# A gated-attention and feed-forward kernel on one core: gate sums worked out once and repeated over partitions by DMA, and attention on TensorE in one run per half block

## The chip, the cores and the metric

One core of a Trainium2 chip. The core has TensorE (matmul; PE in the profile, its weight loads PEld), VectorE (DVE), ScalarE (ACT), GpSimd (POOL) and SyncE (SP), which here only issues DMAs. The metric is device microseconds of one execution. Three runs of the kernel before gave 494.70, 497.48 and 496.63 us, a median of 496.63.

## The reference

A recurrent attention over 4 batches, 8 heads, 768 tokens and a head size of 40, then a feed-forward layer over the 4 x 768 tokens of 320 features, through 2048 hidden units:

```python
for t in range(S):
    m_new = np.maximum(f_gate[:, :, t] + m, i_gate[:, :, t])
    f_stab = np.exp(f_gate[:, :, t] + m - m_new)
    i_stab = np.exp(i_gate[:, :, t] - m_new)
    m = m_new
    C = f_stab * C + i_stab * np.einsum('bhd,bhe->bhde', vt, kt)
    n = f_stab * n + i_stab * kt
    h_tilde = np.einsum('bhde,bhe->bhd', C, qt)
    nq = np.einsum('bhd,bhd->bh', n, qt)[:, :, None]
    y[:, :, t] = sigmoid(o_gate) * h_tilde / np.maximum(np.abs(nq), 1.0)
...
h = x @ w_in
sp = np.maximum(h, 0.0) + np.log1p(np.exp(-np.abs(h)))
return (h * erf(sp)) @ w_out
```

The two weight matrices are double precision; everything else is float32.

## The kernel before

**Attention** works in chunks of L = 128 tokens. There are 6 chunks (c) of 4 batches (b), so 24 steps s = 4c + b. Inside a chunk the recurrence becomes a product of matrices: for tokens t and u with u <= t, the weight of u in t is exp(cum[t] + a[u]) times q[t]k[u], where cum is the running sum of the log of f_stab from the chunk's start and a the rest of the gates' terms. Whatever came before the chunk is in `state`, and enters with the factor exp(cum[t]). The gates of a chunk are worked out by `gate_chunk`: a scan for m (L314), differences on GpSimd (L322, L323), a scan for cum (L329), the rest (L334, L335), an exp (L341), and a split of the results into three bf16 parts (L351 to L353), of which `rhs` lays some on other partitions with twelve small DMAs (L363).

A step's operations, under the names that the code gives them, are: loads of q and k (`load`, L387) and of k, v and the output gate (`loadv`, L393, L394); `rows` (GpSimd, L403) and `pe` (TensorE, L413; L415 too for c = 0), which build cum[t] + a[u] in PSUM out of the bf16 parts; `ex` (ScalarE, L422), two exps of 128x512; `sel` (GpSimd, L427), which clears u > t; `S` (TensorE), which for c > 0 first multiplies `selP` (L443; the prediction calls this part pq) to repeat exp(cum) over partitions, and then forms k q (L449); `vg` (v times the last column of weights); `w` (VectorE, L464); `qa` (VectorE, L473: q times exp(cum)); `ph` (TensorE, L482 to L493: state times q, plus w times v, and, but for the last chunk, the new part of the state); `sa` and `sk` (the state's update); `yg` (VectorE, L524 to L528), `y` and `yy` (GpSimd, L532, L538), which divide and gate; `tr` (TensorE, L544: three transposes); and `xh`, `xl` (L557, L561), which split the transposed result into two parts that TensorE multiplies separately.

**The feed-forward layer** works on blocks of two steps (256 tokens), each in two half blocks; there are 24 such phases f. A phase has four ups (`up`, L675: 16 matmuls of 256 columns) and four downs (`dn`, L737 to L740: 12 of 320), and between them `hb` (copy out of PSUM), `sp` and `er` (softplus and erf on ScalarE), `mu` (VectorE), `gh` and `gl` (a split into two parts). Phases 0 to 3 are blocks 0 and 1, so phase 4 is the first that needs the attention of chunk 1. The weights come as 22 tiles of doubles (`win`, `tail`, `wout`) and are decoded into two float32 parts by `val` (ScalarE), `dec` (VectorE, L580, L581), `hi` (ScalarE, L586) and `lo` (L592, on GpSimd or, where `LO_DVE` names it, on VectorE).

**The order** of all this is written by a planner in the kernel (`Plan`) when the program is built: each operation is given an engine, a cost, what it waits for, which buffers it holds and, for TensorE, a due time. `issue` simulates the engines with these costs and picks, whenever an engine is free, the operation with the least slack. `NUDGE` shifts the slack of single operations, `SLOTS` and `CAPS` count buffers, and `AHEAD` says behind which phase's exps a step's exps stand on ScalarE. The engines then work through their lists strictly in order, and all DMAs go through SyncE's queue in order.

## Time and profile before

| | |
|---|---|
| median of the three runs | 496.63 us |
| profiled execution | 496.05 us, its span 494.3 us |
| instructions | 14040 |
| GpSimd busy | 113.4 us, 23% of the span |
| moved by DMA | 39.40 MB, on average 80 GB/s |
| chain that ended last | TensorE 78%, VectorE 7%, DMA 6%, ScalarE 5% |

The profile is of one execution. A busy time is the sum of an engine's instructions; TensorE's matmuls overlap, so what one costs is read from the distance of starts. The slices cut the span into forty pieces of 12.4 us. The rows on which the prediction rests are shown there.

### The profile page before, as it was taken

The page shows a single profiled execution, that of the slowest core. Times are in us where ns is not written, and L with a number is a line of the kernel's source. Part 1 is how long each engine was busy: PE and PEld are TensorE (multiplying, and loading weights), DVE is VectorE, ACT ScalarE, POOL GpSimd, SP SyncE. Part 2 cuts the span into 40 slices and gives each one's busy share as a digit, 9 for nine tenths or more (in the row PEclk, how much of TensorE's full clock was granted, in tenths as well). Part 3 has the DMA queues.
Part 4 walks back from the last instruction along what each step waited for, and adds up shares of the span by engine and source line. Part 5 has one row for each costly group of instructions (what it writes and reads, how often), then busy time and mean ns, then how long its engine had stood idle before and what let it go on. Part 6 is the DMA issues. An engine that isn't in the chain of part 4 may idle for free.

```text
span 494.3 us, 14040 instructions
## 1 busy us (share of the span) xinstructions
PE 464.1 (94%) x6120; PEld 442.2 (89%) x6120; DVE 327.4 (66%) x562; ACT 333.6 (67%) x412; POOL 113.4 (23%) x187
## 2 busy tenths in 40 slices
PE   2787869799999999999999999999999999999997
PEld 1677769689999999999999999999999999999997
DVE  3787978587685666957675975765864754755541
ACT  4568898985494696567575666666656666667571
POOL 6684453242511011111011211001111001000000
PEclk9998989859999999999999999999999999999999
DMA  7999926123051203212203033203020000000000
GB/s 212 265 324 255 216 92 223 36 77 103 5 174 57 76 7 101 75 43 73 76 16 91 2 93 89 76 16 91 0 88 19 1 15 15 2 15 15 1 27 28
DMA packets 21221, 39.40 MB, mean 80 GB/s; under 512 B 3304, under 2 KB 12520, under 8 KB 21160
## 3 DMA queue, kind: packets, MB, share of 16 engines
q1 hardware_dynamic: 21160, 38.51, 27.2%
q8 instruction: 48, 0.79, 0.7%
q14 instruction: 13, 0.11, 0.1%
HBM read 34.45 MB, written 3.93 MB: 78 GB/s over the span
## 4 chain that ended last, share of the span: by engine, by line
PE 78%; DVE 7%; DMA 6%; ACT 5%; issue 2%; SPq 1%; POOL 0%; ACTq 0%; DVEq 0%
PE h L675 31%; PE po L737 12%; PE po L740 11%; PE po L738 11%; PE pa L449 4%; PE pa L482 3%; PE pa L486 2%; DMA raw<-in_w_out_dram 2%; DMA qk<-in_qk_dram 2%; DVE bits L580 2%; DVE bits L581 2%; PE pa L413 2%; PE pa L544 1%; DMA raw<-in_w_in_dram 1%; PE pa L493 1%
## 5 line engine op out<-in xcount | busy, mean ns | idle before, releaser
L675 PE MATMUL h<-xh,wh 128*128 128x256 f32 x576 | 164.2, 293 | 3.6 <-ACT wh L586 2.4
L675 PE MATMUL h<-xl,wh 128*128 128x256 f32 x576 | 159.7, 285 | 1.3 <-DVE xl L561 1.3
L737 PE MATMUL po<-woh,gh 128*128 128x320 f32 x384 | 119.7, 323 | 0.9 <-ACT woh L586 0.9
L675 PEld LDWEIGHTS h<-xh,wh 128*128 128x128 f32 x576 | 111.7, 194 | 6.7 <-ACT wh L586 2.6
L738 PE MATMUL po<-wol,gh 128*128 128x320 f32 x384 | 114.8, 311 | 1.2 <-POOL wol L592 1.2
L675 PEld LDWEIGHTS h<-xl,wh 128*128 128x128 f32 x576 | 111.8, 194 | 1.9 <-DVE xl L561 1.5
L675 PE MATMUL h<-xh,wl 128*128 128x256 f32 x384 | 109.8, 286 | 1.3 <-POOL wl L592 1.3
L686 DVE COPY hb<-h 128x512 f32<-128x512 f32 x72 | 49.6, 689 | 65.5 <-PE h L675 65.4
L694 ACT ACTIVATE e<-hb 128x1024 f32<-128x1024 f32 x48 | 50.0, 1056 | 63.3 <-DVE hb L686 45.8
L737 PEld LDWEIGHTS po<-woh,gh 128*128 128x128 f32 x384 | 72.8, 190 | 4.4 <-ACT woh L586 1.2
L675 PEld LDWEIGHTS h<-xh,wl 128*128 128x128 f32 x384 | 74.5, 194 | 1.6 <-POOL wl L592 1.6
L738 PEld LDWEIGHTS po<-wol,gh 128*128 128x128 f32 x384 | 72.9, 190 | 1.5 <-POOL wol L592 1.4
L740 PE MATMUL po<-woh,gl 128*128 128x320 f32 x384 | 72.4, 311 | 0.0
L702 DVE TENSOR_TENSOR hb<-e,hb 128x1024 f32<-128x1024 f32 x48 | 57.6, 1225 | 21.3 <-ACT e L698 20.7
L427 POOL TENSOR_SCALAR_AFFINE_SELECT dm<-dm 128x512 f32<-128x512 f32 x48 | 30.8, 663 | 139.3 <-ACT dm L422 139.1
L707 ACT ACTIVATE gh<-hb 128x1024 fp32r<-128x1024 f32 x48 | 50.6, 1058 | 16.3 <-DVE hb L702 15.8
L740 PEld LDWEIGHTS po<-woh,gl 128*128 128x128 f32 x384 | 60.8, 189 | 0.0
L712 DVE TENSOR_TENSOR gl<-hb,gh 128x1024 fp32r<-128x1024 f32 x48 | 59.2, 1236 | 1.5 <-ACT gh L707 1.4
L532 POOL TENSOR_TENSOR kvo<-kvo,den 128x320 f32<-128x320 f32 x24 | 21.7, 906 | 128.9 <-DVE kvo L528 128.8
L698 ACT ACTIVATE e<-e 128x1024 f32<-128x1024 f32 x48 | 48.7, 1052 | 0.3
L694 ACT ACT_TABLE_LOAD x25 | 32.1, 1283 | 4.1 <-DVE hb L686 3.7
L464 DVE TENSOR_TENSOR dm<-pa,dm 128x512 f32<-128x512 f32 x48 | 30.9, 683 | 5.1 <-PE pa L449 4.1
(78 smaller groups left out, 607.3 us busy)
## 6 DMA issues: line engine op xcount, KB each, us to landing
...
raw<-in_w_in_dram SPq DMA_DIRECT2D x8, 512.0 KB
...
```

Source lines behind the costliest of these rows:

```text
L427: nc.gpsimd.affine_select(out=v.w[j], in_=v.w[j], pattern=[[0, NPR], [1, L]], compare_op=ALU.is_ge, fill=0.0, base=0, channel_multiplier=-1)
L464: nc.vector.tensor_tensor(v.w[j], v.ps[j], v.w[j], op=ALU.mult)
L675: nc.tensor.matmul(V.h[i][:, n % 2 * T:(n % 2 + 1) * T], w, m, start=(q == 0), stop=(q == len(ops) - 1))
L686: nc.vector.tensor_copy(V.hb[:, i * 512:(i + 1) * 512], V.h[i])
L694: nc.scalar.activation(V.e, V.hb, AF.Softplus)
L698: nc.scalar.activation(V.e, V.e, AF.Erf)
L702: nc.vector.tensor_tensor(V.hb, V.e, V.hb, op=ALU.mult)
L707: nc.scalar.activation(V.gh, V.hb, AF.Copy)
L712: nc.vector.tensor_tensor(V.gl, V.hb, V.gh.bitcast(F32), op=ALU.subtract)
L737: nc.tensor.matmul(K.po[b], V.gh[:, ts], woh[:, w], start=start, stop=False)
L738: nc.tensor.matmul(K.po[b], V.gh[:, ts], wol[:, w], start=False, stop=False)
L740: nc.tensor.matmul(K.po[b], V.gl[:, ts], woh[:, w], start=False, stop=stop)
```

## The change

- The gates of chunks 1 to 5 are worked out once, on 32 partitions (one for a batch and head) and 768 columns: `lscan`, `lg`, `lsum`, `lrest`, `gexp`. cum and exp(cum) are written to DRAM (`cum_dr`, `dec_dr`). a is transposed by five matmuls (`at`) into `aT`, with tokens on partitions. Chunk 0 keeps its own gates and its `pe`; the clearing of u > t is added there as a matmul of a mask.
- For c > 0 `pe`, `rows`, `rhs`, and the product with `selP` are gone. `bq` reads 8 rows of cum into all 128 partitions (`dm`, 512 KB), and `dq` reads exp(cum) into 104 (`dq`, 208 KB). `add` on GpSimd adds a, then come one exp and one select over 1024 columns.
- `ph` puts its new state's part in the PSUM bank of its output.
- From step 8 on, `merge` makes one TensorE operation of tr of step s - 2, S of step s and ph of step s - 1, so S is one run ahead of its own ph.
- The planner's costs for TensorE's changes from one kind of work to another, its due times, the order of exps on ScalarE (`CHAIN` in place of `AHEAD` and `GATE`), the choice of engine for some operations (`HB_ACT`, `LO_DVE`, `VG_POOL`, `SK_ACT`, new `GL_POOL`), the buffers and `NUDGE` are changed.

```diff
-FIRST = 30.8
-PHASE = 18.0
-BEHIND = 1.3
+FIRST = 11.8
+PHASE = 17.5
+BEHIND = 1.32
...
-HB_ACT = {0, 1, 2, 3, 4, 6}
+HB_ACT = {0, 4, 6}
...
-LO_DVE = {'i01', 'i30', 'i31', 'o0', 'o2', 'o6'}
+LO_DVE = {'o1', 'o6', 't0'}
+CHAIN = [
+    ('ex', 0, 0), ('ex', 0, 1), ('ex', 1, 0), ('ex', 1, 1), ('ex', 2, 0), ('ex', 2, 1), ('ex', 3, 0), ('ex', 3, 1),
...
+GL_POOL = {2, 4}
+CLUSTER = 8
+PREFER = 16.6
...
+    @make('lscan', 'DVE', 3.2, after=[lload, p_small], new=[gmb], use=[gib, gfb])
+    def lscan():
+        late.m = row("late")
+        nc.vector.tensor_copy(late.m[:, 0:1], m0[0:R])
+        nc.vector.tensor_tensor_scan(out=late.m[:, 1:S + 1], data0=late.f[:, 0:S], data1=late.i[:, 0:S], initial=m0[0:R],
+                                     op0=ALU.add, op1=ALU.max)
...
+    @make('lsum', 'DVE', 3.2, after=[lg, p_lones], new=[gcb], use=[gfb, gyb])
...
+    @make('gexp', 'ACT', 0.85, after=[lsum], use=[gcb, gfb], table=('exp',))
+    def gexp():
+        nc.scalar.activation(late.f[:, 0:S], late.c[:, 0:S], AF.Exp)
+
+    def kept(name, t, src, after, buf):
+        @make(name, 'SP', 0.5, kb=100.0, after=after, use=[buf])
+        def put():
+            nc.sync.dma_start(t.rearrange("c b h l -> (b h) c l"), src()[:, 0:S].rearrange("p (c l) -> p c l", l=L))
+        return put
...
+    @make('at', 'PE', 0.5, after=[lrest, p_ident], new=[atb], use=[gib], mode=3)
+    def at_():
+        late.a = bank(NC - 1, R)
+        for c in range(1, NC):
+            nc.tensor.transpose(late.a[:, c - 1], late.i[:, c * L:(c + 1) * L], ident[0:R, 0:R])
...
+            @make(f'bq{s}', 'SP', 0.5, after=[p_cum], kb=512.0, new=[dmb])
+            def bq():
+                v.dm = new(sb, [128, H, L], F32, "dm")
+                v.w = ofj(v.dm)
+                nc.sync.dma_start(v.dm, cum_dr[c, b:b + 1].to_broadcast([128, H, L]))
+
+            @make(f'dq{s}', 'SP', 0.9, after=[p_dec], kb=208.0, new=[dqb])
+            def dqp():
+                v.dq = new(sb, [128, NPR, L], F32, "dq")
+                for j in range(2):
+                    n = 64 if j == 0 else D
+                    nc.sync.dma_start(v.dq[64 * j:64 * j + n],
+                                      dec_dr[c, b:b + 1].rearrange("o (p j) l -> o j p l", j=2)[:, j].to_broadcast([n, NPR, L]))
+
+            @make(f'add{s}', 'POOL', 2.7, after=[bq, p_at], use=[dmb])
+            def addp():
+                nc.gpsimd.tensor_tensor(v.dm, v.dm, aT[:, c - 1, 8 * b:8 * b + 8].unsqueeze(2).to_broadcast([128, H, L]), op=ALU.add)
...
+    for s in range(CLUSTER, B * NC + 1):
+        plan.merge(f'X{s}', [*([step[s - 2].tr] if s > CLUSTER else []), *([step[s].S] if s < B * NC else []), step[s - 1].ph_])
```

Three places show what moves. TensorE, at S of step 12, before (L443 is the product with selP, L449 is S, L737 and L738 begin a down):

```order
L443 LDWEIGHTS selP
L443 MATMUL pa<-splB_71,selP 128x128
L449 MATMUL pa<-qk 128x128 x8
L737 MATMUL po_3219<-woh,gh 128x320
L738 MATMUL po_3219<-wol,gh 128x320
```

TensorE, at S of step 13, now (L807 ends an up, L674 is tr of step 11, L581 is S of step 13, L614 and L618 begin ph of step 12):

```order
L807 MATMUL h<-xl,wh 128x256
L674 MATMUL pa<-ident,kvo 128x128 x3
L581 MATMUL pa<-qk 128x128 x8
L614 MATMUL pa<-state_78,qk 32x82 x4
L618 MATMUL pa<-kvo,dm 32x41 x8
```

The product with selP is gone, and tr, S and ph stand behind each other where downs and ups stood between them.

SyncE's queue, in the early part, before (L639 loads w_out, L607 w_in, L387 and L393 a step's q, k and v):

```order
L639 DMA raw<-in_w_out_dram 128x256
L639 DMA raw<-in_w_out_dram 128x640
L639 DMA raw<-in_w_out_dram 128x128
L607 DMA raw<-in_w_in_dram 128x1024
L387 DMA qk<-in_qk_dram 104x1024
L393 DMA kvo<-in_kvo_dram 128x648
```

SyncE's queue, at the like place, now (L459 writes cum and exp(cum) to DRAM, L543 and L550 are the repeated reads, L771 and L739 load weights, L501 and L502 a step's k and v):

```order
L459 DMA cum_dr<-late 32x6x128
L459 DMA dec_dr<-late 32x6x128
L771 DMA raw<-in_w_out_dram 128x128
L771 DMA raw<-in_w_out_dram 128x640
L771 DMA raw<-in_w_out_dram 128x256
L739 DMA raw<-in_w_in_dram 128x1024 x2
L501 DMA kvo<-in_kvo_dram 128x648
L502 DMA kvo<-in_kvo_dram 128x320
L543 DMA dm<-cum_dr 128x1024
L550 DMA dq<-dec_dr 64x4x128
L550 DMA dq<-dec_dr 40x4x128
```

Weight loads that had other loads ahead of them now have two writes of results ahead of them, and further weights have repeated reads ahead.

GpSimd, before, around a chunk's change (L334 and L335 are gate sums, L427 is sel, L532 y, L538 yy):

```order
L334 TENSOR_TENSOR x_1843<-gt,m_c 128x128
L335 TENSOR_TENSOR x_1843<-x_1843 128x128
L427 AFFINE_SELECT dm<-dm 128x512 x2
L532 TENSOR_TENSOR kvo<-kvo,den 128x320
L538 COPY kvo<-kvo 128x64
```

GpSimd now, around step 7 (L589 is vg, L564 sel, L662 y, L668 yy, L555 the add):

```order
L589 TENSOR_TENSOR vg<-kvo,dm 128x328
L564 AFFINE_SELECT dm<-dm 128x1024
L662 TENSOR_TENSOR kvo<-kvo,den 128x320
L668 COPY kvo<-kvo 128x64
L555 TENSOR_TENSOR dm<-dm,aT 128x1024
```

The gate sums are gone, and each step has an add over 1024 columns.

More of the change, by code (lines that the diff above doesn't have):

```diff
@@ L283, in p_zeros, with p_ones @@
             nc.gpsimd.memset(t, 0.0)
[L285 to L294 removed]
+    @make('ones', 'ACT', 0.95, after=[p_cst])
+    def p_ones():
+        nc.scalar.activation(rhsE, cst[:, 0:8].unsqueeze(2).to_broadcast([128, H, L]), AF.Copy)
@@ new lines, in split @@
+    @make('split', 'DVE', 2.1, after=[rest, p_cst], use=[firstb])
+    def split():
+        x, spl = first.x, first.spl
+        for m in (nm1, nm2):
+            nc.vector.tensor_copy(spl, x)
+            nc.vector.scalar_tensor_tensor(out=x, in0=spl, scalar=m, in1=x, op0=ALU.mult, op1=ALU.add)
+        nc.vector.tensor_scalar(out=spl, in0=x, scalar1=pm, scalar2=pa, op0=ALU.mult, op1=ALU.add)
+    late = SimpleNamespace()
+    R = B * H
+    gib, gfb, gmb, gyb, gcb = (Buf('late') for _ in range(5))
@@ L370, in attention @@
         k, half = divmod(s, NB)
-        v, G = step[s], gate[c]
+        v = step[s]
         prev = step[s - B] if c else None
```

363 lines of the change are left out of this document (199 added, 164 removed), and 70 rows, old and new, of tables (CHAIN, NUDGE).

## Prediction

> **What bounds the kernel now.** I read the page first (engine totals, then the slices), then the table of busy time by stage, then TensorE's instructions in order of time.
>
> ```profile
> span 494.3 us, 14040 instructions
> PE 464.1 (94%) x6120; PEld 442.2 (89%) x6120; DVE 327.4 (66%) x562; ACT 333.6 (67%) x412; POOL 113.4 (23%) x187
> PE   2787869799999999999999999999999999999997
> 0.00:31.00 31.00, 16.77 (x394) 13.25 (x395) 18.56 (x44) 16.90 (x30) 20.78 (x44) 1.00 0.94 261
> 67.00:85.00 18.00, 16.92 (x121) 16.74 (x122) 14.89 (x21) 15.77 (x28) 6.70 (x7) 0.91 0.66 213
> 85.00:103.00 18.00, 14.10 (x211) 12.18 (x209) 10.85 (x19) 17.83 (x24) 8.51 (x9) 0.81 0.16 47
> 229.00:247.00 18.00, 18.00 (x261) 17.28 (x260) 12.04 (x21) 9.74 (x12) 2.37 (x4) 1.00 0.26 81
> ```
>
> The kernel has two parts. Until about 105 us (the first nine slices) TensorE has gaps and in 85 to 103 us runs at a granted clock of 0.81; there weights are loaded and decoded and ScalarE is the fullest engine (17.83 of 18.00). After that TensorE is busy 18.00 of 18.00 at clock 1.00 and nothing else comes near. In the second part, time is what TensorE is given to do. So the sum needs the price of each kind of TensorE work, and the moment at which the second part begins.
>
> In the next rows (start, duration, engine, line) the distance from one start to the next is the price, since matmuls overlap.
>
> ```profile
> 209.64 0.28 PE L675 MATMUL h<-xh,wh 128*128 128x256 f32 x1
> 211.56 0.31 PE L737 MATMUL po<-woh,gh 128*128 128x320 f32 x1
> 213.32 0.28 PE L675 MATMUL h<-xh,wh 128*128 128x256 f32 x1
> ...
> 220.84 0.61 PE L413 MATMUL pa<-rhsE,splB 128*128 128x512 bf16 x2
> ...
> 221.40 0.28 PE L675 MATMUL h<-xl,wh 128*128 128x256 f32 x1
> ```
>
> ```profile
> 194.66 0.40 PE L443 MATMUL pa<-splB,selP 128*128 128x128 bf16 x4
> 194.99 1.16 PE L449 MATMUL pa<-qk 40*128 40x128 f32 x16
> 196.08 0.55 PE L544 MATMUL pa<-ident,kvo 128*128 128x128 f32 x3
> 196.39 0.36 PE L675 MATMUL h<-xh,wh 128*128 128x256 f32 x1
> ...
> 200.23 0.35 PE L482 MATMUL pa<-state,qk 104*32 104x82 f32 x8
> ...
> 201.43 0.49 PE L493 MATMUL pa<-vg,kvo 128*32 128x41 f32 x32
> 201.85 0.39 PE L675 MATMUL h<-xh,wh 128*128 128x256 f32 x1
> 202.07 0.28 PE L675 MATMUL h<-xl,wh 128*128 128x256 f32 x1
> ...
> 241.84 0.40 PE L443 MATMUL pa<-splB,selP 128*128 128x128 bf16 x4
> ...
> 260.63 0.40 PE L443 MATMUL pa<-splB,selP 128*128 128x128 bf16 x4
> ```
>
> One up (16 matmuls) costs 211.56 - 209.64 = 1.92 us, 0.12 a matmul; one down 213.32 - 211.56 = 1.76. A phase has four of each: 14.72 us. The same point of two steps is 260.63 - 241.84 = 18.79 apart, so a step's attention costs 4.07 us of TensorE. Its parts: pe 221.40 - 220.84 - 0.12 = 0.44; the part of S on selP (I call it pq) 0.33; S itself 1.09; tr 0.31; ph 1.62, of which the last 0.42 (from 201.43) make the new state, and 0.10 more before the second matmul of the up behind it (202.07 - 201.85 - 0.12). That adds up to 3.89; the other 0.18 goes in further changes from one kind of work to another.
>
> **The change part by part.** *Removed from TensorE:* pe (0.44) and pq (0.33) in the 20 steps with c > 0. *Moved:* tr, S and ph, which stood in three or four places of a phase, stand in one run from step 8 on, so TensorE changes over once in and once out. The order on TensorE at steps 12 and 13 is shown with the change: pq is gone, and tr, S and ph follow each other where downs and ups stood between. A run costs tr 0.31 + S 1.09 + ph 1.62 + leaving 0.10 = 3.12; I take 3.15 (bounds 3.0, where a change inside the run costs nothing and tr's first matmul hides, and 3.3, with the whole 0.18 left). That is 0.92 less than 4.07 for each step.
>
> *The second part.* Let T be the start of the first up of phase 4. The order has the same 16 ups and 12 downs ahead of it in both kernels, so 80 ups and 84 downs follow: 153.6 + 147.8 = 301.4 us. Before, T is in the chain of waits, and TensorE's last work ends where the last output copy begins:
>
> ```profile
> 117.43 3.83 PE h L675 x32
> 491.03 0.44 ACT L758 ACTIVATE o_sb<-po 128x320 f32<-128x320 f32 x1 [1.32 <-PE po L740]
> ```
>
> 491.0 - 117.4 = 373.6 leaves 72.2 for attention. In the changed order S4 to S7, ph4 to ph6, tr4 and tr5 are ahead of T. What follows: 12 whole runs of 3.15 (37.8), the first without tr (2.8), three whose ph makes no state (3 x 2.73 = 8.2), the last without S (1.6), and two lone tr (0.7): 51.1. The tail from the last down to the end stays 494.3 - 491.0 = 3.3. So the span is T + 301.4 + 51.1 + 3.3 = T + 355.8, where before it was T + 376.9.
>
> *The first part.* What stands before T before:
>
> ```profile
> 44.14 0.38 PE L675 MATMUL h<-xl,wh 128*128 128x256 f32 x1 [1.34 <-DVE xl L561]
> 91.90 0.40 PE L443 MATMUL pa<-splB,selP 128*128 128x128 bf16 x4
> ...
> 94.15 1.16 PE L449 MATMUL pa<-qk 40*128 40x128 f32 x14 [1.44 <-ACT dm L422]
> 97.60 0.59 PE L413 MATMUL pa<-rhsE,splB 128*128 128x512 bf16 x1 [1.97 <-DVE qk L473]
> ```
>
> At 91.9 all 16 ups and 8 downs are done, and S4 begins. The 25.5 us to T hold S4, S5, ph4, ph5, two tr, three pe and four downs, 15.5 us by the prices above; 10 us are waits and the low clock. The change puts S4 behind 8 ups and 4 downs, so chunk 1's chain fills gaps that are there. If 16 ups and 8 downs end at 91.9 again and nothing waits, T is 91.9 + 4 x 1.09 + 3 x 1.72 + 4 x 1.76 + 0.66 = 109.1. Three things push it:
>
> The late gates are one chain, and TensorE's five transposes for aT stand ahead of the ups of phase 1. Prices from:
>
> ```profile
> L314 DVE TENSOR_TENSOR_SCAN m_c<-gt,m_c 128x128 f32<-128x128 f32 x3 | 1.5, 500 | 0.0
> L592 POOL TENSOR_TENSOR wol<-bits,woh 128x512 fp32r<-128x512 f32 x7 | 10.3, 1476 | 19.3 <-ACT woh L586 19.3
> L427 POOL TENSOR_SCALAR_AFFINE_SELECT dm<-dm 128x512 f32<-128x512 f32 x15 | 9.2, 634 | 61.3 <-ACT dm L422 61.3
> L684 ACT ACTIVATE hb<-h 128x512 f32<-128x512 f32 x16 | 9.3, 587 | 1.6 <-PE h L675 1.6
> q1 hardware_dynamic: 21160, 38.51, 27.2%
> ```
>
> Six times as long rows: two scans of 6 x 0.50 = 3.0 us, four GpSimd operations of 1.5 x 1.48 = 2.2: about 15 us in series. The gate rows stand behind 6.3 MB of loads, 24 us at 261 GB/s, so the chain ends at 43 to 47 us, 0 to 3 behind the 44.1 at which those ups started. Behind it wait the cum_dr and dec_dr writes, and on SyncE's queue everything after them. In the rows of SyncE shown with the change, the tile of w_in that came ahead of the loads of a step now has two writes ahead of it, and further on two tails, two more w_in tiles and five w_out units wait behind two to three steps' repeated rows: 1.9 MB, 7 us at 261 GB/s. The DMA engines had a third free in 67 to 85 us (0.66), so most of it hides; if tile slots force the order it is up to 7 us. Against that, ScalarE has about 5 us less ahead of T: three phases' hb copies (12 x 0.59 = 7) go to VectorE and two fills with ones go, against gexp, the mask and two exps more. (VectorE has them to carry: it was busy 10.85 of 18 in 85 to 103.) I take T = 113: the 109.1 plus 4. Bounds: 104 (109.1 less the 5 us of ScalarE) and 124 (117.4 plus the 7).
>
> *A repeated row's price* is in no row. The queue's share is 0.272 x 16 x 494.3 / 21160 = 0.10 us of one engine for a packet; by packets the 128 + 416 of a step take 3.4 us, by bytes 720 KB at 261 GB/s 2.8. With the step's own loads (0.26 of 18 us, 4.7) that is 8 of a 17.9 us phase: hidden behind TensorE. GpSimd's rows with the change show one add a step more: 2 x 1.48 = 3.0 us, and GpSimd's 2.37 us of the window 229 to 247 becomes 5.4 of 17.9 (vg is on GpSimd in early steps alone). VectorE loses the gate work and keeps about 12 of 17.9; ScalarE's one exp of 1024 replaces two of 512. All of it is hidden in the second part, as long as a step's w, yg and xl end within the phase between two runs.
>
> What speaks against the add:
>
> ```profile
> 58.38 1.50 POOL L592 TENSOR_TENSOR wh<-bits,wh 64x512 fp32r<-64x512 f32 x1 [1.82 <-ACT wh L586]
> 58.62 1.53 DVE L580 TENSOR_SCALAR bits<-bits 128x512 int32<-128x512 int32 x1
> 60.19 0.69 DVE L581 SCALAR_TENSOR_TENSOR bits<-raw,bits 128x512 int32<-128x512 int32 x1
> 69.93 0.41 DVE L580 TENSOR_SCALAR bits<-bits 128x512 int32<-128x512 int32 x1
> ```
>
> Alone L580 takes 0.41; started under a GpSimd operation it took 1.53 and ended 0.27 behind that one. So an add of 3.0 can hold a VectorE operation up to 3 us. That is the mechanism of the first rival. The Trainium skill (SBUF — State Buffer, Who interferes with whom) says that the two share one pair of ports as an exclusive lock, taken by VectorE's operations in a 2-port mode and, against a GpSimd operation that reads, by those with two SBUF inputs. By that rule mu, gl, vg, qa and sa would all be held too, GpSimd's 5.4 us would count in full beside VectorE's 12, and 17.4 of 17.9 would leave no room: rival 1, 487.5; the row agrees for L580, and shows nothing on the others.
>
> **Sum.** 113 + 355.8 = 468.8 span, and 496.05 - 494.3 = 1.75 around it: 470.5 us. The profiled execution's 496.05 is 0.6 under the median of the runs shown, 496.63.
>
> **Rivals.** (1) *The run waits.* TensorE works in order, so a run starts when the latest of its parts is ready, and ups and downs queue behind it; before, tr, S and ph could wait apart. The parts' feeders (xl, w, yg) stand on VectorE behind operations that an add can hold. For it: 3.0 us at a time. Against it: VectorE has 6 us of a phase free, and a run's feeders have a phase. At 1 us a run, 17 runs: 487.5. (2) *The first part gains nothing or grows*: the gate chain or the loads behind it come late, T = 121, 478.5. For it: the queue rows above. Against it: a third of the DMA time was free. (3) *The first part gains more*: T = 105, 462.5; for it, ScalarE's fewer operations and 10 us of waits and low clock between 91.9 and 117.4. (4) *The repeated reads are slow, and the kernel slower than before.* 128 partitions read the same 4 KB, which no row shows. With 4.7 us for its own loads, a step's transfers reach the old pitch of 18.8 when 720 KB take 14 us, 51 GB/s, a fifth of 261. From there each phase is as long as its transfers: at 40 GB/s, 18 + 4.7 = 22.7, and 20 steps lose 20 x (22.7 - 17.9) = 96: 566. Against it: nothing seen so far moved that slowly for its size. (5) *The change doesn't do what it says*: pq and pe are gone from the order, that is certain; but if S and ph cost more in a run (weights of 40 and of 104 rows directly behind each other) by all that was saved, 0.9 us x 17, the time is 486.
>
> **How the numbers follow.** Forecast, 463 to 478 us: 0.52. Rivals 1, 2 and 5 between 478 and 494: 0.26. Rival 3, under 463: 0.12. Within 0.5% of 496.63 (494.1 to 499.1; about what a measurement of this kernel can tell from no change): 0.04, where rivals 1 and 2 meet. Slower, by rival 4: 0.06. So faster 0.90. The range: low, T = 104 with runs of 3.0 (355.8 - 2.4), 457.4 + 1.75 = 459; high, T = 124 and 0.3 us of waiting a run, 479.8 + 5.1 + 1.75 = 487. It leaves out about 0.06 below and 0.14 above.
>
> **What would show it.** Right: the distance between two S in the second part is 17.9 (18.79 before), with no wait of TensorE on a run, and the first up of phase 4 starts at about 113. Wrong, in the second part: TensorE waiting at L674, L581 or L614, on VectorE (rival 1) or on DMA behind dm or dq (rival 4), or a run longer than 3.3 without a wait (rival 5). Wrong, in the first: the five transposes of L471 later than 47, the last weight decoded later than the 104 us of before, or a granted clock under 0.8 over more of it. A GpSimd add of more than 3.0 would be a mis-sized term without effect on the sum.

## The result, and the profile after

| | before | after |
|---|---|---|
| time, median of 20 runs (us) | 497.16 | 494.28 |
| lowest and highest | 494.50, 499.54 | 491.86, 496.09 |
| span of the profiled execution | 494.3 | 491.2 |
| T, the first up of phase 4 | 117.4 | 135.4 |
| from T to the end of the span | 376.9 | 355.8 |

The ratio after to before is 0.9932, 95% interval 0.9915 to 0.9950: the kernel is 0.7% faster, where 470.5 us, 5% faster, was predicted, with a range of 459 to 487. The second part came out as forecast, to the tenth of a microsecond: T + 355.8. The first part did not: T was to be 113 and is 135.4. What the second part gained, 21.1 us, the first part lost again but for 3. One execution of a later run, e9, took 1085.84 us and is left out of what is said of e9.

The page of the kernel after: span, TensorE, VectorE and GpSimd in all, and TensorE's 40 slices.

```profile
span 491.2 us, 13646 instructions
PE 449.3 (91%) x6013; PEld 433.4 (88%) x6013; DVE 344.1 (70%) x493; ACT 332.6 (68%) x383; POOL 175.3 (36%) x150
PE   1696863997999999999999999999999999999997
```

Before, the row with gaps had nine slices; now it has ten, and they are emptier. TensorE's own work fell by 15 us (464.1 to 449.3), GpSimd's grew by 62 (113.4 to 175.3).

The table of busy time by stage after: window, its length, then busy us of PE, PEld, DVE, ACT, POOL (with counts), the granted clock, the DMA share and GB/s.

```profile
31.00:49.00 18.00, 13.91 (x268) 12.48 (x267) 16.79 (x23) 8.74 (x18) 14.65 (x10) 0.78 0.93 281
49.00:67.00 18.00, 12.86 (x96) 11.95 (x96) 14.55 (x20) 15.75 (x22) 8.16 (x7) 0.96 0.89 258
67.00:85.00 18.00, 9.38 (x60) 8.67 (x59) 16.12 (x14) 14.05 (x16) 13.10 (x8) 0.80 0.61 187
85.00:103.00 18.00, 16.30 (x218) 15.70 (x219) 17.76 (x24) 9.07 (x17) 11.54 (x9) 0.82 0.44 140
229.00:247.00 18.00, 18.00 (x261) 17.65 (x260) 15.14 (x24) 17.64 (x20) 5.55 (x5) 1.00 0.41 125
```

The window of 49 to 67 us before, which the argument also needs:

```profile
49.00:67.00 18.00, 13.12 (x90) 12.02 (x89) 16.66 (x22) 16.16 (x23) 8.78 (x9) 1.00 0.68 156
```

In 85 to 103 us the fullest engine was ScalarE (17.83) before; now it is VectorE (17.76, from 10.85). GpSimd has 13.10 and 11.54 in the two windows where it had 6.70 and 8.51. In the second part TensorE stays at 18.00 of 18.00.

TensorE in order of time after (start, duration): two starts of S that follow each other, a run with its parts, the first matmul behind it, and, from the chain of waits, the first up of phase 4.

```profile
164.86 1.16 PE L581 MATMUL pa<-qk 40*128 40x128 f32 x16
182.70 1.16 PE L581 MATMUL pa<-qk 40*128 40x128 f32 x16
...
232.37 0.49 PE L674 MATMUL pa<-ident,kvo 128*128 128x128 f32 x3
232.79 1.16 PE L581 MATMUL pa<-qk 40*128 40x128 f32 x16
233.88 0.35 PE L614 MATMUL pa<-state,qk 104*32 104x82 f32 x8
...
235.08 0.48 PE L623 MATMUL pa<-vg,kvo 128*32 128x41 f32 x32
235.49 0.41 PE L869 MATMUL po<-woh,gh 128*128 128x320 f32 x1
```

```profile
135.46 4.58 PE h L807 x37
```

The distance between two S is 182.70 - 164.86 = 17.84 (17.9 predicted, 18.79 before), and a run takes 235.49 - 232.37 = 3.12 (3.15 taken). No row in the second part shows TensorE waiting. So the question is what made the first part 18 us longer than before, and 22 longer than predicted.

What VectorE does from 67 us on in the kernel after (the first rows), and GpSimd beside it (the second):

```profile
67.23 0.68 DVE L818 COPY hb<-h 128x512 f32<-128x512 f32 x1
68.77 2.27 DVE L713 SCALAR_TENSOR_TENSOR bits<-raw,bits 128x512 int32<-128x512 int32 x1
70.96 2.92 DVE L844 TENSOR_TENSOR gl<-hb,gh 128x1024 fp32r<-128x1024 f32 x1
75.34 2.27 DVE L713 SCALAR_TENSOR_TENSOR bits<-raw,bits 128x512 int32<-128x512 int32 x1
```

```profile
68.41 4.38 POOL L555 TENSOR_TENSOR dm<-dm,aT 128x1024 f32<-128x1024 f32 x2
72.76 2.27 POOL L724 TENSOR_TENSOR wl<-bits,wh 128x512 fp32r<-128x512 f32 x1
74.98 2.08 POOL L555 TENSOR_TENSOR dm<-dm,aT 128x1024 f32<-128x1024 f32 x1
```

L713 takes 0.69 us alone (it is the operation that was L581 before). Here it takes 2.27, each time beside an add on GpSimd. VectorE's groups up to T (total us, mean ns, and the engine's idle time before them), after:

```profile
L713 DVE SCALAR_TENSOR_TENSOR bits<-raw,bits 128x512 int32<-128x512 int32 x22 | 26.5, 1205 | 0.8
L712 DVE TENSOR_SCALAR bits<-bits 128x512 int32<-128x512 int32 x22 | 16.5, 752 | 6.6 <-ACT bits L707 6.6
L818 DVE COPY hb<-h 128x512 f32<-128x512 f32 x12 | 8.2, 683 | 2.3 <-PE h L807 2.3
```

and before:

```profile
L581 DVE SCALAR_TENSOR_TENSOR bits<-raw,bits 128x512 int32<-128x512 int32 x22 | 18.1, 821 | 0.8
L580 DVE TENSOR_SCALAR bits<-bits 128x512 int32<-128x512 int32 x22 | 15.4, 698 | 3.3 <-ACT bits L575 3.1
```

22 x 0.69 is 15.2, so the first row of after holds 11.3 us of stretch, where before it held 2.9. I call stretch what an instruction takes beyond the shortest of its line and shape in the same trace. Added up over all of VectorE's instructions up to T, it is 14 us before and 33 after. By what stands beside them on GpSimd, the 33 us are: the subtractions of the decoding (L724) 12.5, the adds (L555) 6.8, the low halves on GpSimd (L844) 3.6, the late gates 4.0, the rest some 6. An operation often stands beside two of these, so each share is good to about 1 us only. Besides, VectorE has the 12 copies of row L818, 8.2 us.

The chain that ended last, followed back from the end of the span, passes through VectorE as well: of the 59 us from 62.8 to 121.7 us, 37.3 are VectorE's, 11.0 ScalarE's, 1.8 GpSimd's; the rest is DMA and issue, and TensorE has none. Three of its pieces (start, us, what), the last of them the first of TensorE:

```profile
115.23 2.58 DVE vg L589
119.61 2.05 DVE qk L603
121.79 0.50 PE pa L614 x8
```

### The profile page after: what moved, and what is told of

It reads as the page before. It is cut to its first block, busy times and chain, and to the rows that moved or that the text cites. A ratio compares the mean times of both kernels' runs of the same rounds, so it can differ in the third digit from the quotient of the medians.

```text
span 491.2 us, 13646 instructions
## 1 busy us (share of the span) xinstructions
PE 449.3 (91%) x6013; PEld 433.4 (88%) x6013; DVE 344.1 (70%) x493; ACT 332.6 (68%) x383; POOL 175.3 (36%) x150
## 4 chain that ended last, share of the span: by engine, by line
PE 76%; DMA 10%; DVE 8%; ACT 3%; issue 2%; POOL 1%; SPq 1%; DVEq 0%; ACTq 0%; POOLq 0%
PE h L807 32%; PE po L869 11%; PE po L872 11%; PE po L870 11%; DMA raw<-in_w_in_dram 4%; PE pa L581 4%; PE pa L614 3%; DMA raw<-in_w_out_dram 3%; DVE bits L713 3%; PE pa L618 2%; DMA dq<-dec_dr 2%; PE pa L674 1%; DVE bits L712 1%; DVE gl L844 1%; PE pa L623 1%
## 5 line engine op out<-in xcount | busy, mean ns | idle before, releaser
L807 PE MATMUL h<-xh,wh 128*128 128x256 f32 x576 | 158.3, 285 | 1.3 <-DVE hb L818 0.9
L807 PE MATMUL h<-xl,wh 128*128 128x256 f32 x576 | 157.5, 283 | 1.6 <-DVE xl L692 1.6
L807 PEld LDWEIGHTS h<-xh,wh 128*128 128x128 f32 x576 | 109.6, 190 | 2.3 <-DVE hb L818 1.4
L807 PEld LDWEIGHTS h<-xl,wh 128*128 128x128 f32 x576 | 109.7, 190 | 1.8 <-DVE xl L692 1.8
L807 PE MATMUL h<-xh,wl 128*128 128x256 f32 x384 | 109.1, 284 | 2.2 <-POOL wl L724 2.2
L662 POOL TENSOR_TENSOR kvo<-kvo,den 128x320 f32<-128x320 f32 x24 | 25.3, 1052 | 179.4 <-DVE kvo L658 179.4
L818 DVE COPY hb<-h 128x512 f32<-128x512 f32 x84 | 57.6, 686 | 41.4 <-PE h L807 40.8
L834 DVE TENSOR_TENSOR hb<-e,hb 128x1024 f32<-128x1024 f32 x48 | 65.4, 1372 | 14.6 <-ACT e L830 14.6
L807 PEld LDWEIGHTS h<-xh,wl 128*128 128x128 f32 x384 | 73.1, 190 | 2.4 <-POOL wl L724 2.4
L844 DVE TENSOR_TENSOR gl<-hb,gh 128x1024 fp32r<-128x1024 f32 x44 | 63.1, 1435 | 5.5 <-ACT gh L839 5.1
L555 POOL TENSOR_TENSOR dm<-dm,aT 128x1024 f32<-128x1024 f32 x20 | 48.2, 2409 | 18.3 <-DMA dm<-cum_dr 18.3
L654 DVE TENSOR_SCALAR den<-pa 128x8 f32<-128x8 f32 x24 | 3.9, 165 | 55.2 <-PE pa L623 41.8
```

Source lines behind the costliest of these rows:

```text
L555: nc.gpsimd.tensor_tensor(v.dm, v.dm, aT[:, c - 1, 8 * b:8 * b + 8].unsqueeze(2).to_broadcast([128, H, L]), op=ALU.add)
L662: nc.gpsimd.tensor_tensor(v.y[:, 0:DM].rearrange("p (h d) -> p h d", d=D), v.th.rearrange("p (h d) -> p h d", d=D), v.den.unsqueeze(2).to_ ...
L807: nc.tensor.matmul(V.h[i][:, n % 2 * T:(n % 2 + 1) * T], w, m, start=(q == 0), stop=(q == len(ops) - 1))
L818: nc.vector.tensor_copy(V.hb[:, i * 512:(i + 1) * 512], V.h[i])
L834: nc.vector.tensor_tensor(V.hb, V.e, V.hb, op=ALU.mult)
L844: (nc.gpsimd if f in GL_POOL else nc.vector).tensor_tensor(V.gl, V.hb, V.gh.bitcast(F32), op=ALU.subtract)
```

## The theories

**V:** VectorE is the bound of the first part, because GpSimd's new work stretches it and the 12 copies were given to it. **Q:** SyncE's queue and the transfers are the bound: 8 small loads of the late gates (line 416), the two writes that wait for the gate sums (line 459), and the repeated rows stand ahead of the weights. **W:** weight tiles come late, since SyncE waits for a tile slot. **G:** the late gates' chain, by its place on SyncE, VectorE and TensorE ahead of the first MLP phases, sets the start. All edits are made in the parts' bodies, so that the planner's order stays, unless a run says otherwise.

| run | T | stretch before T | time | ratio to before, 95% interval |
|---|---|---|---|---|
| the kernel after | 135.4 | 33 | 494.28 | 0.9932 [0.9915, 0.9950] |
| e1 gates in two loads | 137.5 | 32 | 493.12 | 0.9921 [0.9895, 0.9948] |
| e2 add of one head | 133.1 | 25 | 490.70 | 0.9860 [0.9845, 0.9875] |
| e3 copies on ScalarE | 132.1 | 29 | 490.46 | 0.9860 [0.9844, 0.9877] |
| e4 writes early | 136.0 | 33 | 493.79 | 0.9925 [0.9908, 0.9941] |
| e5 = e2 + e3 | 130.5 | 22 | 488.45 | 0.9816 [0.9788, 0.9843] |
| e6 exponent per head | 136.1 | 24 | 493.67 | 0.9914 [0.9886, 0.9942] |
| e7 adds on VectorE | 133.4 | 27 | 491.32 | 0.9871 [0.9844, 0.9899] |
| e8 decoding on VectorE | 135.1 | 18 | 492.72 | 0.9896 [0.9864, 0.9929] |
| e9 late gates on VectorE | 136.0 | 28 | 493.80 | 0.9903 [0.9868, 0.9939] |
| **e10 GpSimd's load on VectorE, copies on ScalarE** | 127.1 | 5 | **485.94** | 0.9780 [0.9738, 0.9822] |
| e11 attention apart | 136.1 | 33 | 497.00 | 0.9995 [0.9968, 1.0022] |
| e12 repeats of one head | 135.1 | 32 | 493.13 | 0.9909 [0.9865, 0.9953] |
| e13 = e10, four tiles at hand | 127.4 | 5 | 485.78 | 0.9752 [0.9728, 0.9776] |
| e14 four tiles at hand alone | 135.6 | 33 | 493.48 | 0.9902 [0.9873, 0.9931] |
| e15 = e10 + e1 | 127.9 | 5 | 485.95 | 0.9757 [0.9732, 0.9781] |
| e16 = e10, tile ahead of gates | 133.8 | 6 | 491.73 | 0.9885 [0.9850, 0.9919] |
| e17 tile ahead of gates alone | 144.2 | 30 | 498.86 | 1.0023 [1.0001, 1.0046] |
| e18 = e10 without late gates | 122.7 | 6 | 479.81 | 0.9640 [0.9597, 0.9683] |

T and the stretch are read from the one profiled execution of each run, the time is the median of 4 to 10 executions (20 of the kernel after). Executions of one kernel lie 1 to 7 us apart, so a difference in T of under 1 us between two runs is not told from chance. The kernel before was run beside each, with medians of 497.0 to 498.4 us, and the ratio goes by these. T + 355.8 gives the span of e10 (482.9) exactly and that of e18 (478.7) within 0.3.

## Experiments: SyncE's queue and the transfers

**e1, the late gates in two loads.**

```diff
-        for b in range(B):
-            for t, x in ((late.i, 0), (late.f, 1)):
-                nc.sync.dma_start(t[8 * b:8 * b + 8, 0:S], gates[32 * b:32 * b + 8, x])
+        src = gates.rearrange("(b r) x s -> b r x s", r=32)
+        for t, x in ((late.i, 0), (late.f, 1)):
+            nc.sync.dma_start(t[0:R, 0:S], src[:, 0:H, x])
```

> The 8 small loads of the late gates (line 416) become 2 loads of the same bytes; the result is the same. Theory Q (SyncE's queue: the late gates and the waiting writes stand ahead of the weight loads): the queue waited 8.4 us in all at these 8 loads, and the DMA share fell to 0.28 at 28 to 30 us; that hole closes, the first ups of phase 1 (52.98 us) come 4 to 8 us earlier, T (135.4) 4 to 8 us earlier, and the time is 486 to 490. Theory V (VectorE is the bound of the first part: GpSimd's adds hold it and it has the 12 hb copies): the early ups gain, but VectorE's 16 to 17.8 busy of 18 from 67 to 121 us stay; T moves by under 2 us, time 492.5 to 494.5.

Measured: 493.12 us, and T later, not earlier (137.5, in the slowest of the four executions). The queue's rows after had looked like a plain cause, 8 small loads that keep SyncE for 10.48 us:

```profile
18.24 10.48 SPq L416 DMA_DIRECT2D late<-in_gates_dram  x8
```

In e1 the two loads are issued in 2.84 us, yet the w_in tile behind them is issued at 27.64, 1.6 us sooner only: SyncE then waited for the transfers in flight. The DMA share in 13 to 31 us rises from 0.84 to 0.96, and T gains nothing by it. Theory Q loses its first part.

**e4, the writes not waiting for the gate sums.**

```diff
-            nc.sync.dma_start(t.rearrange("c b h l -> (b h) c l"), src()[:, 0:S].rearrange("p (c l) -> p c l", l=L))
+            nc.sync.dma_start(t.rearrange("c b h l -> (c b) (h l)"),
+                              gates.rearrange("p x s -> (p x s)")[0:NC * B * H * L].rearrange("(a l) -> a l", l=H * L))
```

> The two writes to DRAM (line 459) take their data from the gates in DRAM as they lie there, and so don't wait for the late gate sums: the decay is computed from other numbers, and all else stays. Theory Q: the queue's wait of 5.5 us at 42.6 to 48.4 us goes, the weight loads behind it come 4 to 6 us earlier, T 3 to 5 us earlier, time 489 to 491.5. Theory V: T within 1 us, time 493.5 to 495.

Measured: 493.79 us, T 136.0. The cum_dr write is issued at 44.14 us in place of 48.45 and the w_out tiles behind it at 46.41 in place of 49.71, but the w_in tiles behind those at 51.30 and 51.23, and T doesn't gain.

**e12, the repeats cut to a sixth.**

```diff
-                nc.sync.dma_start(v.dm, cum_dr[c, b:b + 1].to_broadcast([128, H, L]))
+                nc.sync.dma_start(v.dm[:, H - 1:H], cum_dr[c, b:b + 1, 0:1].to_broadcast([128, 1, L]))
...
-                nc.gpsimd.tensor_tensor(v.dm, v.dm, aT[:, c - 1, 8 * b:8 * b + 8].unsqueeze(2).to_broadcast([128, H, L]), op=ALU.add)
+                nc.gpsimd.tensor_tensor(v.dm, v.dm[:, H - 1:H].to_broadcast([128, H, L]), aT[:, c - 1, 8 * b:8 * b + 8].unsqueeze(2).to_broadcast([128, H, L]), op=ALU.add)
```

and the same for dq.

> The reads of the repeated rows bring one head of eight (and one pair of four), and the other heads use the same numbers: 116 KB a step in place of 720; all other work and the order stay. Theory Q (transfers hold the first part): the DMA engines are busy 0.89 in 49 to 67 us, and 1.8 MB or 7 us of it goes: the weights behind come 3 to 7 us earlier, T falls by 3 to 6 us, time 488 to 491.5. Theory V: T within 1.5 us, time 492.5 to 495.

Measured: 493.13 us, T 135.1. The windows of e12:

```profile
49.00:67.00 18.00, 12.86 (x87) 11.73 (x86) 14.05 (x17) 14.70 (x21) 8.15 (x6) 0.91 0.58 183
85.00:103.00 18.00, 16.61 (x225) 15.58 (x226) 17.73 (x24) 9.11 (x15) 11.55 (x9) 0.90 0.35 104
```

The DMA share in 49 to 67 us falls from 0.89 to 0.58, and VectorE's 17.7 in 85 to 103 stays. The transfers were busy, but cutting these to a sixth left T where it was. With e1 and e4, each part of theory Q has been tried alone and none brought T forward, and with Q goes the prediction's rival of slow repeated reads.

## Experiments: VectorE and GpSimd

**e2, the add of one head in eight, and e3, the copies back on ScalarE.**

```diff
-                nc.gpsimd.tensor_tensor(v.dm, v.dm, aT[:, c - 1, 8 * b:8 * b + 8].unsqueeze(2).to_broadcast([128, H, L]), op=ALU.add)
+                nc.gpsimd.tensor_tensor(v.dm[:, 0:1], v.dm[:, 0:1], aT[:, c - 1, 8 * b:8 * b + 1].unsqueeze(2).to_broadcast([128, 1, L]), op=ALU.add)
```

```diff
-                    if f in HB_ACT:
+                    if f in HB_ACT or f < 4:
```

> GpSimd adds the key's value to one head of eight (128x128 in place of 128x1024), the other seven are left without it; every wait and the order stay. Theory V: the four adds before T last 2.1 to 2.3 us each, 8.8 together, and what VectorE runs beside them is stretched (L713 2.28 in place of 0.69, gl 2.92 in place of 1.2); T falls by 4 to 7 us, time 487.5 to 490.5. Theory Q: nothing of the queue is changed; T within 1 us, time 493.5 to 495.

> The 12 copies of the hidden block of phases 1, 2 and 3 go back from VectorE to ScalarE, at their places in the order; the result is the same. Theory V: VectorE loses 12 x 0.68 = 8.2 us, ScalarE gets 12 x 0.58 = 7.0 (it is busy 14 to 17 of 18 in 49 to 85 and 103 to 121, 9 in 85 to 103); T falls by 4 to 8 us, time 486.5 to 490.5. Theory Q: T within 2 us either way, time 492.5 to 496.

Measured: 490.70 and 490.46 us, T 133.1 and 132.1. Both move as theory V says, but T moves by 2.3 and 3.3 where at least 4 was expected of each. e3 takes work off VectorE alone; e2 also shortens GpSimd's own work.

**e5, both together.**

> The edits of the runs with one head added (seven heads of eight are left without the key's value) and with the 12 copies on ScalarE together. Theory V: they take two separate loads off VectorE (T fell by 2.3 and 3.3 us alone), so the times add: T 128.5 to 131, time 486 to 488.5. If they relieve the same wait, or ScalarE is the bound once the copies are back, the time is that of the better one alone, 489.5 to 491.

Measured: 488.45 us, T 130.5. The two add up in the main: 3.6 and 3.8 us alone, 5.8 together.

**e6, the add as the bias of ScalarE's exponent.**

```diff
-                nc.gpsimd.tensor_tensor(v.dm, v.dm, aT[:, c - 1, 8 * b:8 * b + 8].unsqueeze(2).to_broadcast([128, H, L]), op=ALU.add)
-                nc.scalar.activation(v.dm, v.dm, AF.Exp)
+                for n in range(H): nc.scalar.activation(v.dm[:, n], v.dm[:, n], AF.Exp, bias=aT[:, c - 1, 8 * b + n:8 * b + n + 1])
```

> The add on GpSimd goes; ScalarE adds the key's value as the bias of its exponent, 8 instructions of 128x128 per step in place of one of 128x1024; the result is the same. Theory V: as with one head added, VectorE is held 6 to 8 us less before T, but ScalarE takes about 1.2 us more for each step by its fixed part (8 x 0.28 against 1.06): T 132 to 134.5, time 490 to 493. If ScalarE's chain is the bound instead, 4 steps x 1.2 = 5 us are added to T and the time is 496 to 500.

Measured: 493.67 us, T 136.1: neither case. VectorE's stretch fell by 9 us, about as in e2. ScalarE's busy time rose from 14.05 to 16.33 us in 67 to 85 us and from 16.96 to 17.69 in 103 to 121, so its longer exponents probably took the gain back; that was not tried apart.

**e7, the adds of steps 4 to 7 on VectorE, and e8, the decoding's subtractions on VectorE.**

```diff
-                nc.gpsimd.tensor_tensor(v.dm, v.dm, aT[:, c - 1, 8 * b:8 * b + 8].unsqueeze(2).to_broadcast([128, H, L]), op=ALU.add)
+                (nc.vector if s < 8 else nc.gpsimd).tensor_tensor(v.dm, v.dm, aT[:, c - 1, 8 * b:8 * b + 8].unsqueeze(2).to_broadcast([128, H, L]), op=ALU.add)
```

```diff
-            e = nc.vector if engine == 'DVE' else nc.gpsimd
+            e = nc.vector
```

> The adds of steps 4 to 7 are made by VectorE in place of GpSimd; the result is the same. Theory V in the form that GpSimd's work stretches VectorE's: in the trace the instructions of VectorE that stand beside these adds are 6.8 us longer than their shortest kind, and the adds themselves would take VectorE 4 x 1.2 = 4.9: T falls by 1 to 3 us, time 491 to 493.5. If the stretch costs nothing and VectorE's own work is the bound, T grows by 4 to 5 us and the time is 498 to 499.

> The 19 subtractions of the weight decoding that GpSimd makes (line 724) go to VectorE; the result is the same. Beside them VectorE's instructions are 12.5 us longer than their shortest kind in the trace; on VectorE they take 19 x 0.69 = 13.1. Theory V (stretch): VectorE's load is the same within 1 us, the low halves come sooner (0.69 in place of 1.3 to 2.5): T moves by -4 to +1, time 490 to 495. If the stretch costs nothing, T grows by 8 to 13 us, time 502 to 507.

Measured: e7 491.32 us, T 133.4; e8 492.72 us, T 135.1. These two show that the stretch costs time. VectorE got some 5 us of adds in e7 and 13 us of subtractions in e8, and T did not grow by 4 to 5 and 8 to 13 us, as it would have if VectorE's own work alone counted: the stretch fell by 6 and by 15. GpSimd's doing this work had been no saving for VectorE.

**e9, the late gates' steps on VectorE.** Lines 428 to 430 and 450 go from `nc.gpsimd` to `nc.vector`.

> The four GpSimd subtractions and additions of the late gates (lines 428 to 430 and 450, 7.1 us in all) go to VectorE; the result is the same. In the trace wl (line 724) stands behind them on GpSimd and TensorE waits 2.2 us for it, and the transposes of line 471 begin at 52.1 us. Theory V with GpSimd's order as a part of it: beside them VectorE is stretched by 4.0 us and the work itself is about 3.5 there, so VectorE's load is the same, wl comes up to 4 us sooner, the transposes start at 47 to 50, T falls by 2 to 5 us, time 489.5 to 492.5. If the late gates don't set the start of phase 1, T moves by under 1 us, time 493.5 to 495.

Measured: 493.80 us, T 136.0. TensorE no longer waits for wl and phase 1 starts at 51.3 in place of 53.0, but by T nothing of it is left. In the profiled execution, then, 2 us at the start are worth nothing, with VectorE full behind it (17.73 of 18 in 85 to 103 us). That execution took 494.07 us; three of the nine took 488.9 to 490.7, and no trace shows what these three did.

**e10, all of it: e7, e8 and e9, the low halves of phases 2 and 4 on VectorE, and the copies on ScalarE (e3).**

> Adds of steps 4 to 7, the subtractions of the weight decoding, the low halves of phases 2 and 4 and the late gates' steps go from GpSimd to VectorE, and the 12 copies of the hidden block to ScalarE; the result is the same. Theory V (stretch): of the 33.2 us by which VectorE's instructions before T are longer than their shortest kind, about 26 go; 24 of work come and 8.2 of copies leave: VectorE's load before T is about 104 us in place of 114.4, near the 100.0 of the run with one head added and the copies on ScalarE (T 130.5): T 129 to 133, time 487 to 491. If the stretch cost nothing, VectorE would have 16 us more than in the changed kernel, and the time is over 500.

Measured: **485.94 us**, T 127.1: 8.3 us better than the kernel after, 2.2% better than before. Among the versions that compute the right result it is the fastest, level with e15. It also came out better than its expectation (487 to 491 us, T 129 to 133), which went by VectorE's load alone: that is about 104 us up to T, more than e5's 100, and yet T is 3.4 us earlier than in e5. The chains show a second thing that left with GpSimd's work. In e5, from 60.7 to 116.8 us, the chain that ended last has 9.3 us of GpSimd's own subtractions (L724), for which other engines wait; in e10, from 59.7 to 113.9, it has nothing of GpSimd. So part of the 8.3 us is GpSimd's slower results and not VectorE's stretch; no run parts the two. Its VectorE at the place shown above, and two of its groups up to T:

```profile
68.32 1.22 DVE L555 TENSOR_TENSOR dm<-dm,aT 128x1024 f32<-128x1024 f32 x1
...
69.91 0.69 DVE L713 SCALAR_TENSOR_TENSOR bits<-raw,bits 128x512 int32<-128x512 int32 x1
70.52 1.22 DVE L844 TENSOR_TENSOR gl<-hb,gh 128x1024 fp32r<-128x1024 f32 x1
```

```profile
L713 DVE SCALAR_TENSOR_TENSOR bits<-raw,bits 128x512 int32<-128x512 int32 x22 | 16.1, 730 | 0.8
...
L555 DVE TENSOR_TENSOR dm<-dm,aT 128x1024 f32<-128x1024 f32 x4 | 4.9, 1218 | 0.0
```

The add takes 1.22 us on VectorE; on GpSimd it took 2.1 on average and stretched VectorE by 1.7 each (6.8 over 4). L713's mean is 730 ns in place of 1205. The stretch before T is about 5 us in place of 33. The windows of e10:

```profile
67.00:85.00 18.00, 10.12 (x61) 9.74 (x62) 16.45 (x21) 17.79 (x24) 1.09 (x1) 0.74 0.66 205
103.00:121.00 18.00, 16.35 (x251) 15.54 (x250) 12.69 (x22) 17.88 (x24) 5.05 (x6) 1.00 0.29 82
```

ScalarE is the fullest in both, 17.79 and 17.88, as it was in 85 to 103 us before the change. T is 127.1 all the same, where it was 117.4 before: 10 us are still to be found.

## Experiments: the second part, and the rest of the first

**e11, no runs.** `CLUSTER` is 25 in place of 8, so that tr, S and ph stay parts of their own and the planner places them.

> No runs are formed: tr, S and ph of a step stay parts of their own and the planner places them; the result is the same, the order changes throughout. For the second part: without pe and pq a step's attention is 4.07 - 0.77 = 3.30 by the prediction's prices, against 3.12 in a run, so the distance between two S grows from 17.84 to 18.0 to 18.05, or stays at 17.84 if the run gains nothing. The time moves by 3 us for that, and by what the other order makes of T, which no theory gives: 492 to 502.

Measured: 497.00 us, T 136.1. S in the second part of e11:

```profile
205.97 1.16 PE L581 MATMUL pa<-qk 40*128 40x128 f32 x16
224.03 1.16 PE L581 MATMUL pa<-qk 40*128 40x128 f32 x16
```

The distance is 18.06 (18.04 to the next), against 17.84 with runs. So of the 0.95 us by which a phase got shorter, about 0.74 come from pe and pq, and 0.2 from the runs. By time (497.00 against 494.28) the runs are worth some 3 us in all.

**e13 and e14, four weight tiles at hand** (e13 on e10, e14 on the kernel after).

```diff
-            raw_tile(v)
-            for i in range(2):
+            if part > 1: v.raw = wh[:, 0, 0:1024].bitcast(I32)
+            else: raw_tile(v)
+            for i in range(2 if part < 2 else 0):
```

and the same for two tiles of w_in.

> The kernel with GpSimd's load on VectorE, in which moreover four of the 22 weight tiles (the two tails and two w_in tiles that SyncE issues at 70.7 to 74 us) are not loaded: their decoding reads a decoded part of wh instead, with the same instructions. Theory W (weights come late: after 62.7 us SyncE waits 8.9 us for a tile slot, and ScalarE decodes no tile between 68 and 79 us): the four are decoded 8 to 11 us earlier and those behind them are issued earlier, T falls from 127.1 by 4 to 9 us, time 477 to 482. If VectorE or ScalarE is what remains (17.8 of 18 on ScalarE in 67 to 85 us), T falls by under 2 us, time 484 to 486.5.

> The same four tiles not loaded, in the changed kernel itself with GpSimd's load left as it was. Theory W as the first cause: T falls by 4 to 9 us, time 485 to 490. Theory V as the first cause: VectorE is busy 16 to 17.8 of 18 from 67 us on, the tiles at hand only queue there: T falls by 0 to 3 us, time 491.5 to 494.5.

Measured: e13 485.78 us, T 127.4; e14 493.48 us, T 135.6. A window of e13:

```profile
67.00:85.00 18.00, 10.01 (x62) 9.44 (x61) 16.46 (x21) 17.72 (x23) 1.09 (x1) 0.74 0.46 147
```

2 MB less are moved, the DMA share in this window falls from 0.66 to 0.46, and VectorE and ScalarE stand as in e10. The tiles were there at once and were decoded when their turn came. Theory W is out for these four tiles.

**e15, e10 with the gates in two loads.**

> The kernel with GpSimd's load on VectorE and the late gates in 2 loads in place of 8; the result is the same. With VectorE relieved the early loads could set the pace: if they do, T falls by 2 to 5 us from 127.1, time 481 to 484. If not, T and time stay, 484.5 to 487.5.

Measured: 485.95 us, T 127.9: nothing, also with VectorE relieved, though the DMA share in 13 to 31 us rises from 0.83 in e10 to 0.99.

**e16 and e17, a tile ahead of the gates** (e16 on e10, e17 on the kernel after). The order is changed by hand after planning:

```diff
+    ahead('win10', 'lload')
+    for n in ('val', 'dec', 'hi', 'lo'):
+        ahead(n + 'i10', 'vali11')
+    ahead('lg', 'lsum')
+    for n in ('cumw', 'decw'):
+        ahead(n, 'bq4')
...
```

> The kernel with GpSimd's load on VectorE, with a few places in the order changed by hand and the result the same: the w_in tile of phase 0's third and fourth up is loaded ahead of the late gates and decoded ahead of its two sister tiles; the late gates' subtractions stand behind it and behind step 3's w; the five transposes stand behind the ups of phase 1, and the two writes to DRAM behind three weight tiles. Theory G (the late gates stand ahead of the first MLP phases, and ScalarE, which is idle 18 of the 36 us from 13 to 49, never gets that time back): the ups of phase 0 don't wait, the first up of phase 1 comes from 53.6 to 47 to 50 us, the first softplus from 55.4 to 49 to 52, and T falls from 127.1 by 3 to 6 us: time 480 to 483. If the start of the MLP isn't what T hangs on, T moves by under 1.5 us, time 484.5 to 487.5.

> The same places changed in the changed kernel itself, with GpSimd's load left as it was; the result is the same. Theory G as a cause of its own: T falls from 135.4 by 3 to 6 us, time 488 to 491. Theory V as the one bound: VectorE is full from 67 us on, whatever comes earlier waits there: T falls by under 2 us, time 492.5 to 495.

Measured: 491.73 and 498.86 us, 5.8 and 4.6 us worse, T 133.8 and 144.2, 6.7 and 8.8 us later: the opposite of both cases. (e17's trace is of the slowest of its ten executions, 501.90 us.) In e16 ScalarE waits 1.84 us for the tile and 1.22 for its bits, with two exponents of the decay queued behind them; the second transposes start at 33.7 in place of 31.2, and phase 1 at 54.1. The move put 3 us of new waits at the head of ScalarE's queue, so it says nothing of theory G.

**e18, e10 without the late gates' chain.**

```diff
-                nc.sync.dma_start(t[8 * b:8 * b + 8, 0:S], gates[32 * b:32 * b + 8, x])
+            nc.gpsimd.memset(t[:, 0:S], 0.0)
...
-        nc.vector.tensor_tensor_scan(out=late.m[:, 1:S + 1], data0=late.f[:, 0:S], data1=late.i[:, 0:S], initial=m0[0:R],
-                                     op0=ALU.add, op1=ALU.max)
...
-        nc.vector.tensor_tensor_scan(out=late.c[:, 0:S], data0=late.one[:, 0:S], data1=late.f[:, 0:S], initial=0.0,
-                                     op0=ALU.mult, op1=ALU.add)
+        nc.gpsimd.memset(late.c[:, 0:S], 0.0)
```

> The kernel with GpSimd's load on VectorE, without the late gates' chain: their 8 loads, both scans and the steps between are left out (GpSimd fills the rows with zeros instead), and everything that uses the rows, and the order, stays. Theory G (the chain's place and work in the first 54 us is the rest of the lateness): 8.2 us of VectorE's work before 50 us go, SyncE has no 10.5 us of small loads at 18 to 29 us, the transposes don't wait, the first up of phase 1 comes from 53.6 to 46 to 50 us, T falls from 127.1 by 4 to 8 us, time 478 to 482. If the rest lies in how the other work is ordered: the early ups gain, but T falls by under 2 us, time 484 to 487.

Measured: 479.81 us, T 122.7: 6.1 us of time and 4.4 of T less than e10. The transposes in the kernel after, then the transposes and the first up of phase 1 in e10, and then in e18:

```profile
52.12 0.49 PE L471 MATMUL pa<-ident,late 32*128 32x32 f32 x5
```

```profile
52.73 0.49 PE L471 MATMUL pa<-ident,late 32*128 32x32 f32 x5
53.59 0.38 PE L807 MATMUL h<-xh,wh 128*128 128x256 f32 x1 [0.37 <-ACT xh L688]
```

```profile
46.09 0.49 PE L471 MATMUL pa<-ident,late 32*128 32x32 f32 x5
46.96 0.39 PE L807 MATMUL h<-xh,wh 128*128 128x256 f32 x1 [0.38 <-ACT xh L688]
```

and the window of e18 that answers to the first one shown of after:

```profile
31.00:49.00 18.00, 15.54 (x297) 13.78 (x296) 14.56 (x32) 12.45 (x24) 3.71 (x6) 0.98 0.96 283
```

ScalarE does 12.45 us of work there (8.68 in e10, 8.74 in the kernel after), and TensorE's granted clock is 0.98 (0.78 in both). Theory G holds for this part: the chain delays the first phases, and in e10 that time isn't got back. What in the chain does it, its place in the queues, its 8.2 us of work on VectorE or TensorE's lower clock beside it, e18 doesn't tell, since it takes all of them out at once. In the kernel after, a 2 us earlier start brought nothing in e9's trace, which suggests that there the chain lay hidden behind VectorE.

**What stays open.** 122.7 is still 5.3 over the 117.4 of before. The first up of phase 0 is late, at 34.9 us in e18 and 35.65 after, where before it was:

```profile
29.48 0.38 PE L675 MATMUL h<-xh,wh 128*128 128x256 f32 x1
```

In the kernel after, ScalarE and TensorE at that place show

```profile
22.77 0.63 ACT L718 ACTIVATE wh<-bits 128x512 fp32r<-128x512 f32 x1 [2.23 <-DVE bits L713]
23.31 0.58 ACT L535 ACTIVATE dm<-pa 128x512 f32<-128x512 f32 x1
```

```profile
25.56 0.29 PE L618 MATMUL pa<-kvo,dm 128*32 128x41 f32 x3 [3.48 <-issue]
```

an exponent that stands behind a weight's copy, whose VectorE operation comes late, and TensorE idle for 3.48 us. This reading was argued from the rows and not tried by a run. Nor was another: up to 46 us the loads take 80% of the chain that ended last in the kernel after and 65% before.

## Why the prediction was right or wrong, point by point

- **The second part: right.** Pitch 17.84 (17.9), run 3.12 (3.15), T + 355.8 (T + 355.8), no wait on a run. That the sum meets to the tenth is luck: 17 runs shorter by 0.03 are 0.5 us, which something else makes up for. Rivals 1 and 5 did not come: VectorE was busy 15.14 of 18 in the window shown, not 12, and ScalarE 17.64, yet each run's feeders had a phase's time and came in time. A GpSimd add took 1.9 to 2.3 us up to T and 1.9 to 3.7 behind it, where 3.0 was taken, without effect on the second part.
- **The repeated reads: right.** They were priced at 7 us of DMA time in the first part, mostly hidden. Cutting them to a sixth left T where it was (e12). Rival 4 did not come.
- **"I take T = 113: the 109.1 plus 4": this is the step that failed**, by 22.4 us, beyond its bound of 124. Its base was that "16 ups and 8 downs end at 91.9 again and nothing waits", and three terms were to be added to it:
  - *VectorE's load was not a term at all.* The prediction showed from a row that L580 takes 1.53 in place of 0.41 under a GpSimd operation, and used that for the runs of the second part alone. In the first part VectorE's decoding of 22 tiles, gl, mu, vg and qa are stretched beside GpSimd's adds, subtractions and late gates: 33 us of stretch against 14. The copies were waved through with "busy 10.85 of 18 in 85 to 103", the emptiest 18 us up to T; VectorE had been busy 16.66 in 49 to 67. Taking GpSimd's load off GpSimd and the copies off VectorE gave 8.3 us of T (e10), the adds alone 2.3 (e2), the copies alone 3.3 (e3).
  - *The rule was at hand.* The Trainium skill (SBUF — State Buffer, Who interferes with whom) says which VectorE operations GpSimd holds, and the prediction applied it to the second part, where there was room. The trace agrees with it: L713 with two SBUF inputs goes from 0.69 to 2.27 us, vg (L589) from 0.48 to 2.65.
  - *The gate chain "ends at 43 to 47 us, 0 to 3 behind the 44.1":* the transposes of L471 began at 52.1, where the prediction had called anything past 47 a sign of being wrong. Its own parts were cheaper than taken (the scans 2.90 and 1.74 us for 6.0, GpSimd's four steps 7.1 for 8.9). What it stood behind, and what stood behind it on each engine, was missing. Taken out of e10, it gave 4.4 us of T (e18).
  - *"ScalarE has about 5 us less" was no help*, since the fullest engine had become VectorE.
  - *The other two signs came too.* The last L713 of the decoding ends at 115.2 us, where its like before, L581, ended at 102.2. The granted clock was 0.79 and 0.78 in 13 to 31 and 31 to 49 us, before 1.00 and 0.91. The clock is not what held the kernel from 62.8 to 121.7 us, where TensorE isn't on the chain. Ahead of that, the chain has 30 matmuls of the ups in 6.13 us, 0.20 each where the prediction's price is 0.12: some 2.5 us, an estimate, that no run parts from the rest.
- **The sum of what the runs show:** 117.4 to 135.4 is 18.0. Taken out in this order, 8.3 go with GpSimd's load and the copies and 4.4 with the late gates; 5.3 are open. That the first up starts 6.2 us later may be part of them, which no run tried. Each of the three is the difference of two single executions.
- **Rival 2 was the right one** in kind ("the first part gains nothing or grows"), but for a reason it didn't name, and far too small: T = 121 there, 8 over the forecast, where it came 22 over.
